# Attention with a top-1 mixture of experts on one core: maxima exchanged in full between the two heads, subtracted with one product per part and head, and a third maxima job moved in three iterations

## The chip, the cores and the metric

The kernel runs on one core of a Trainium2 chip. The metric is device time in microseconds for one execution, inputs and outputs in the chip's main memory. The engines are PE (matrix products), DVE (vector work), ACT (activations and copies), POOL (a general engine, which here also issues some transfers) and SP (which issues most transfers). "PEld" in the profile is PE's loading of weights, which runs beside its products.

## The reference

Attention over 8 batches, 8 heads, 576 positions and 64 dimensions, with a mask by blocks of 64: a query sees its own block and all earlier ones. The result, seen as rows of 512, goes through a layer in which each row uses one of 8 experts.

```
scores = (q @ k.T) / sqrt(64)
scores = where(block_i >= block_j, scores, -1e9)
scores = scores - max(scores, axis=-1)
attn   = exp(scores);  attn = attn / (sum(attn) + 1e-9)
x      = attn @ v                      # as rows of 512
logits = x @ w_gate;   local = sigmoid(x @ w_local)
e      = argmax(logits[s]) if s == 0 or local[s] < 0.5 else the previous row's e
out[s] = softmax(logits[s])[e] * (relu(x[s] @ w1[e]) @ w2[e])
```

## The kernel before

The attention is a software pipeline over 32 pairs of heads. One pair lies on the 128 partitions, head 0 on 0 to 63 and head 1 on 64 to 127 (a "half" each). In the iteration numbered `it` (L869) pair a = it + 2 is turned (PE transposes queries and keys, L912), pair c = it + 1 gets its scores and exponentials, pair e = it is multiplied with v (`av`), and pair x = it - 1 is normalized, stored, and used for the gate's logits. The order on each engine is written out by hand: an engine takes its instructions in the order of the code, and an instruction that waits holds all behind it.

Scores are made transposed: keys on the partitions, queries along the columns (`products`, L554), in four segments of one or two parts (`SEGS`, L366). A query's maximum therefore has to be subtracted along the columns. It is found beforehand from a low-precision copy of queries and keys (`qh`, `kh`) with queries on the partitions: `top` makes the products and `maxima` reduces them on DVE, in three jobs per pair. Jobs 0 and 1 treat query blocks 6 and 7, 4 and 5, 0 and 1 by pairs of blocks: such a product has block b on partitions 0 to 63 and block b + 1 on 64 to 127, for each head h in a column of its own. Job 2 treats blocks 8, 3 and 2 with `qd`, a block-diagonal arrangement that has head 0 on the lower and head 1 on the upper partitions from the start. All jobs write into the tile `mx`; `PLACE` (L505) says where a block's columns begin.

To subtract, `shift` (L545, on POOL) spreads a column of `mx` over a diagonal (`negi` is minus the identity), and `less` (L558) adds ones-times-diagonal to the scores on PE, which puts minus the maximum of a query in its column on all key partitions. Each half of the partitions serves one head: `lhsT=ones[rows(h)]`, `rhs=diag[rows(h), ...]`.

For jobs 0 and 1 half of the maxima lie on the other head's partitions. L538 copies these to columns 6 to 8 of the right partitions: two copies of 64x3, on DVE (for the first pair on ACT). The diagonals of such blocks are then in two places, the direct ones and the copied ones, in an order that alternates with the head, so that `less` uses separate products: L573 for blocks 2, 3 and 8, and L583 for the others, each half and each of the two places by itself. That makes 34 small products per pair, 22 in the first two segments and 12 in the others; `shift` treats 12 places in three calls (4, 5 and 3).

Around it on DVE: the maxima of job 1 (L535) and the copies (L538) end an iteration; at the head of the next stand the normalization of pair x (`norm`, L481 and L482), what the plan has for "begin", the maxima of job 2 (L543), and the casts into `kh`, `qh` (L928) and `qd` (L939). On PE the head has job 2's products (L526), the eight transposes (L912), the turning of pair x's result (`turn_x`, L620), then scores. Job 2 reads the old `kh` and `qd`, so the casts follow its products. All three jobs share one PSUM tile for their products (`ps_m`): the next job's products wait for the last job's maxima. On POOL the order is: shifts of job 1, the issue of one load of expert weights (L64), shift of job 2, the cast of the result for storing (L464), and tails of `kh` and `qd` (L976, L978).

The routing of the rows (which expert, which place) is done in small steps in the middle of the attention; `plan` (L826) says in which iteration and where. For groups g = 0, 1, 2 the iteration 8g + 11 has "begin" (`ranks_in`), "turn" (`ranks`) and "mid" (`shares`) steps, all on DVE.

After the attention the experts' layer runs over tiles of 128 rows (gather, L744, L756, scatter).

Of the kernel before, what the change touches and what calls it, by code (L numbers as in the profile page):

```python
# [16 lines left out]
def kernel(  # L17
# [11 lines left out]
    nc = tc.nc  # L29
    F32 = mybir.dt.float32  # L30
    BF16 = mybir.dt.bfloat16
# [4 lines left out]
    ALU = mybir.AluOpType  # L36
# [365 lines left out]
    with tc.manual_schedule():  # L402
# [6 lines left out]
        def const(shape, dt, name):  # L409
            return cst.tile(shape, dt, tag=name, name=name)  # L410
# [17 lines left out]
            nc.gpsimd.memset(vt[i][:, :, :, D:D + 1], 1.0)  # L428
            nc.gpsimd.memset(vt[i][64:128, 4], 0.0)

        diag0 = scr[:, 0:12 * 64].rearrange("p (s t) -> p s t", t=64)
        diag1 = const([P, 12, 64], BF16, "diag")
        nats, pls, mxs, xs, xbs, xTs = {}, {}, {}, {}, {}, {}

        def load_qk(i, engs=(nc.sync,)):
# [59 lines left out]
        def rows(h):  # L495
            return slice(64 * h, 64 * h + 64)
# [33 lines left out]
        def maxima(i, job, ps):  # L530
            flat = ps.rearrange("p b c -> p (b c)")
            mx = mxs[i]
            if job < 2:
                for (b, c, n) in PAIRS[job]:
                    nc.vector.reduce_max(mx[:, PLACE[b]:PLACE[b] + 2], ps[:, :, c:c + n], axis=AX)  # L535
                if job == 1:
                    for h in range(2):
                        (nc.vector.tensor_copy if i else nc.scalar.copy)(  # L538
                            mx[rows(h), 6:9], mx[rows(1 - h), h:6:2])
                return  # L540
            for (b, c, n) in FULL:
                z = PLACE[b]
                nc.vector.reduce_max(mx[:, z:z + 1], flat[:, c:c + n], axis=AX)  # L543

        def shift(i, s0, n):  # L545
            nc.gpsimd.tensor_tensor(  # L546
                (diag1 if i else diag0)[:, s0:s0 + n, :], negi[:, None, :].to_broadcast([P, n, 64]),
                mxs[i][:, s0:s0 + n, None].to_broadcast([P, n, 64]), op=ALU.mult)

        def products(i, ps, s, part):  # L550

# [6 lines left out]
        def less(i, ps, s, part):  # L558

            j, a, n, c = SEGS[s][part]  # L560
            diag = diag1 if i else diag0
            blocks = range(a // 64, (a + n) // 64)
            ends = part == len(SEGS[s]) - 1
            for b, w in ((0, 1), (2, 2), (4, 2), (8, 1)):
                if b not in blocks:
                    if b == 4 and 6 in blocks:
                        b, w = 6, 1
                    else:
                        continue
                o, z = c + 64 * b - a, PLACE[b]  # L570
                if b in (2, 8):
                    for h in range(2):
                        nc.tensor.matmul(ps[:, h, o:o + 64 * w], lhsT=ones[rows(h), :],  # L573
                                         rhs=diag[rows(h), z:z + w, :], start=False,
                                         stop=ends and b + w - 1 == blocks[-1])
                    continue
                for e in range(2):
                    for h in range(2):
                        out_s = ps[:, h, o:o + 128 * w].rearrange("p (m e t) -> p m e t", e=2, t=64)
                        zz = slice(z + h, z + h + 2 * w - 1, 2)  # L580
                        if e:
                            zz = slice(6 + z // 2, 6 + z // 2 + w)
                        nc.tensor.matmul(out_s[:, :, e ^ h, :], lhsT=ones[rows(h), :],  # L583
                                         rhs=diag[rows(h), zz, :], start=False,
                                         stop=ends and e == 1 and b + 2 * w - 1 == blocks[-1])

        def seg_tile():
            return ps_sp.tile([P, 2, 512], F32, tag="s", name="ps_s")
# [239 lines left out]
        def at(it, where, f):  # L828
            plan.setdefault((it, where), []).append(f)

        for g in range(3):
            i0 = 8 * g + 9
            at(i0, "turn", lambda ps, g=g: fresh(g))
            at(i0, "turn", lambda ps, g=g: fresh_b(g))
            at(i0, "free", lambda ps: rows_ps(ps, buf))
            at(i0, "mid", lambda ps: scan_rows(plan["free"], buf))
            at(i0, "end", lambda ps: ends_ps(ps, buf))
            at(i0 + 1, "begin", lambda ps: carry(ps, buf))
            at(i0 + 1, "turned", lambda ps: carry_ps(ps, buf))
            at(i0 + 1, "turn", lambda ps: scanned(ps, buf))  # L840
            at(i0 + 1, "first", lambda ps, g=g: chosen_ps(g, ps, buf))
            at(i0 + 1, "mid", lambda ps, g=g: chosen(g, ps))
            at(i0 + 1, "end", lambda ps, g=g: ranks_ps(g, ps))
            at(i0 + 2, "begin", lambda ps: ranks_in(ps))
            at(i0 + 2, "turn", lambda ps, g=g: ranks(g))
            at(i0 + 2, "mid", lambda ps, g=g: shares(g))
            at(i0 + 3, "turn", lambda ps, g=g: ranks_b(g))
            at(i0 + 3, "mid", lambda ps, g=g: shares_b(g))
            at(i0 + 4, "top", lambda ps, g=g: shares_out(g))
            at(i0 + 4, "turn",  # L850
               lambda ps, g=g: low((ohl01[:, GC * g:GC * g + GC, :] if g < 2 else ohl1), GC * g, GC))
# [17 lines left out]
        for it in range(-2, NPR):  # L869
# [11 lines left out]
                                      in_=moe_w_local[ko * P:(ko + 1) * P, :])  # L881

            last_ps = None
            if on_c and c > 0:
                last_ps = top(c, 2, ps_mp) if c > 1 else second
            if last_ps is not None and not on_a:
                maxima(c, 2, last_ps)
                shift(c, 9, 3)
            if on_x:
                norm(x, g0_b, 0, 6)  # L890
            run(it, "top")
            run(it, "begin", ge)
            if last_ps is not None and on_a:
                maxima(c, 2, last_ps)
                shift(c, 9, 3)
            if on_x:
                store_x(x, nc.gpsimd.tensor_copy if it < NPR - 1 else nc.scalar.copy)
            if it == NPR - 1:
# [2 lines left out]
            if on_a:  # L901
                nat = nats[a]
                if a < 3:
                    pw = [g_tile(0), g_tile(1)]
                else:
                    ps = ps_sp.tile([P, 2, 512], F32, tag="s", name="ps_t")
                    pw = [ps[:, 0, :], ps[:, 1, :]]
                pl = pls[a] = plb[:, a % 2]
                mxs[a] = o_p.tile([P, 12], F32, tag="mx", name="mx")
                for w in (1, 0):  # L910
                    for t in range(4):
                        tr = nc.tensor.transpose(pw[w][:, 128 * t:128 * t + 128],  # L912
                                                 nat[:, 4 * w + t].rearrange("p h d -> p (h d)"),
                                                 id_f)
                        if w == 0 and a:

                            tc.declare_no_dep(tr.ins, group="keys", reason="another bank")
                    if a == 0:
                        warm(8 if w else 0)
                        turned(0, w, pw[w])  # L920
                        continue
                    if a < 3:
                        continue
                    cp = nc.scalar.copy(pl[:, w * S:w * S + 512], pw[w])  # L924
                    if w == 1:
                        tc.add_to_no_dep_group("keys", cp.ins)
                    src = pl[:, w * S:w * S + 512]
                    nc.vector.tensor_copy(kh[:, 0:512] if w else qh, src)  # L928
                if a in (1, 2):

                    cast = nc.scalar.copy if a == 1 else nc.vector.tensor_copy
                    cast(kh[:, 0:512], pw[1])
                    cast(qh, pw[0])
                    src = qh
                    for w in (1, 0):
                        nc.scalar.copy(pl[:, w * S:w * S + 512], pw[w])
                if a:
                    for h in range(2):
                        nc.vector.tensor_copy(  # L939
                            qd[rows(h), 0:2, rows(h)],  # L940
                            src[rows(h), 128:256].rearrange("p (b t) -> p b t", t=64))
# [69 lines left out]

            if a == 1:
                maxima(a, 1, top(a, 1, ps_mp))
                shift(a, 0, 4)
                shift(a, 4, 5)
            elif on_a:
                maxima(a, 0, top(a, 0, ps_mp))
            if on_x and not on_a:
# [26 lines left out]
            if on_a:  # L1045
                if a != 1:
                    maxima(a, 1, top(a, 1, ps_mp if a else ps_sp))
                    shift(a, 0, 4)
                    shift(a, 4, 5)
                if a == 0:  # L1050

                    opened = seg_tile()
                    products(a, opened, 0, 0)
                    products(a, opened, 0, 1)
                    maxima(a, 2, top(a, 2, ps_mp))
                    shift(a, 9, 3)
            if it >= 0:

                for _ in range(2 if it in (4, 6) else 1):
# [179 lines left out]
```

## Time and profile before

| | |
|---|---|
| median of 3 runs | 488.1 us (486.54 to 491.87) |
| the profiled execution | 487.98 us, span 486.2 us |
| PE busy | 469.7 us, 97% |
| DVE busy | 343.4 us, 71% |
| POOL busy | 267.5 us, 55% |
| ACT busy | 252.3 us, 52% |
| the products that subtract maxima | L573 x448, L583 x640 |
| shifts on POOL (L546) | 59.5 us x93, and three of the first pair |
| the copies on DVE (L538) | 18.1 us x62 |

The attention takes up to about 330 us of the span, the experts' layer the rest. A steady iteration takes about 9.8 us, and more where the gate's sums or the routing have work in it. The span is the time from the first to the last instruction of the program; the execution's time is 1.8 us longer. A matmul's duration in the profile includes its way through the array, so that the distance from one start to the next, and not the duration, says what it costs.

### The profile page before, as it was taken

What the parts mean: (1) busy time and instruction counts of PE and PEld (TensorE: products, weight loads), DVE (VectorE), ACT (ScalarE), POOL (GpSimd) and SP (SyncE); (2) the same over time, 40 slices, a digit from 0 to 9 for tenths busy, and PEclk for the clock granted to TensorE, in tenths of its full rate; (3) what the DMA queues carried; (4) which work ended last, traced back from release to release, by engine and by line L of the source; (5) the groups of instructions that cost most, each with busy time, mean ns of one, the idle gap of its engine ahead of it and who ended that gap; (6) DMA issues with size and microseconds to landing.
All of it is one profiled execution on the core that took longest, in us unless ns stands there. A gap on an engine that the chain in (4) does not pass through costs nothing.

```text
span 486.2 us, 19978 instructions
## 1 busy us (share of the span) xinstructions
PE 469.7 (97%) x7959; PEld 374.7 (77%) x7980; DVE 343.4 (71%) x868; ACT 252.3 (52%) x512; POOL 267.5 (55%) x477
## 2 busy tenths in 40 slices
PE   8999999999999999999999999999999999999992
PEld 6687888888878888887888887878777777676770
DVE  5688767778898887889877879996468953434330
ACT  4645555455545455554555554544545545555551
POOL 3455444544445554444554345354587778888761
PEclk9999999999999999999999999999999999999997
DMA  7787999997999789787888878634556666667541
GB/s 153 137 179 135 167 171 185 187 158 148 172 165 157 149 156 170 147 162 145 138 164 161 166 142 165 104 60 100 122 152 149 132 151 164 145 150 150 149 115 50
DMA packets 180974, 71.33 MB, mean 147 GB/s; under 512 B 165008, under 2 KB 173200, under 8 KB 180880
## 3 DMA queue, kind: packets, MB, share of 16 engines
q1 hardware_dynamic: 161920, 37.93, 38.4%
q0 software_dynamic: 17760, 31.79, 35.1%
q8 instruction: 66, 1.08, 1.0%
q10 hardware_dynamic: 1200, 0.30, 0.3%
q14 instruction: 28, 0.23, 0.2%
HBM read 67.45 MB, written 14.97 MB: 170 GB/s over the span
## 4 chain that ended last, share of the span: by engine, by line
PE 86%; DVE 6%; DMA 2%; issue 2%; POOL 1%; ACT 1%; POOLq 0%; DVEq 0%; ACTq 0%
PE ps_s L554 18%; PE g L614 15%; PE ps_h L744 13%; PE ps_o L756 12%; PE ps_t L912 5%; PE g L606 4%; PE ps_m L526 3%; PE g L620 3%; PE ps_s L583 3%; PE ps_m L515 3%; DMA out_dram<-o_sb,tok2s 2%; DVE mx L535 2%; PE g L663 2%; PE ps_s L573 2%; DVE mx L543 1%
## 5 line engine op out<-in xcount | busy, mean ns | idle before, releaser
L593 ACT ACTIVATE prob<-ps_s 128x640 f32<-128x640 f32 (+2 forms) x128 | 100.2, 834 | 86.7 <-PE ps_s L573 62.7
L554 PE MATMUL ps_s<-plb 64*128 64x320 f32 (+4 forms) x768 | 105.9, 407 | 0.0
L535 DVE TENSOR_REDUCE mx<-ps_m 128x2 f32<-128x1024 f32 (+2 forms) x96 | 80.2, 864 | 32.3 <-PE ps_m L519 32.1
L546 POOL TENSOR_TENSOR diag<-negi,mx 128x256 bf16<-128x256 f32 (+2 forms) x93 | 59.5, 640 | 52.8 <-DVE mx L535 18.1
L614 PE MATMUL g<-vt,prob 128*64 128x65 f32 x2560 | 87.7, 223 | 0.2 <-issue 0.2
L554 PEld LDWEIGHTS ps_s<-plb 64*128 64x128 f32 x768 | 66.8, 186 | 24.8 <-issue 9.6
L598 POOL MEMSET prob<- 64x128 f32 x128 | 23.9, 200 | 108.5 <-ACT prob L593 108.5
L614 PEld LDWEIGHTS g<-vt,prob 128*64 128x64 f32 x2560 | 80.3, 138 | 3.7 <-issue 0.3
L756 PE MATMUL ps_o<-w_bf,hT 128*128 x283 | 67.4, 379 | 1.7 <-issue 0.7
L748 ACT ACTIVATE hT<-ps_h 128x512 bf16<-128x512 f32 x76 | 45.2, 597 | 19.8 <-PE ps_h L744 19.5
L924 ACT COPY plb<-ps_t 128x512 f32<-128x512 f32 x58 | 31.1, 589 | 42.5 <-PE ps_t L912 42.5
L760 ACT ACTIVATE o_sb<-ps_o,share 128x512 f32<-128x512 f32 x38 | 26.1, 687 | 45.8 <-PE ps_o L756 39.8
L756 PEld LDWEIGHTS <-hT 128*128 128x128 bf16 x304 | 28.3, 98 | 27.8
L543 DVE TENSOR_REDUCE mx<-ps_m 128x1 f32<-128x576 f32 (+2 forms) x96 | 43.0, 503 | 3.8 <-PE ps_m L526 3.6
L720 DVE COPY natb<-w_bf 128x4096 bf16 x20 | 24.6, 1228 | 29.9 <-PE ps_h L744 27.4
L720 DVE COPY plb<-w_bf 128x4096 bf16 x20 | 24.5, 1227 | 26.5 <-PE ps_h L744 25.3
L744 PEld LDWEIGHTS <-natb 128*128 128x128 bf16 x608 | 35.5, 98 | 4.6 <-issue 0.3
L744 PEld LDWEIGHTS <-plb 128*128 128x128 bf16 x608 | 35.5, 98 | 4.4 <-issue 0.3
L766 POOL DMA_INDIRECT out_dram<-o_sb,tok x20 | 30.3, 1517 | 13.2 <-ACT o_sb L760 8.2
L766 POOL DMA_INDIRECT out_dram<-o_sb,tok2s x18 | 30.7, 1704 | 11.6 <-ACTq L1191 4.8
L912 PE MATMUL ps_t<-id_f,natb 128*128 128x128 f32 x232 | 30.1, 273 | 0.0
L583 PEld LDWEIGHTS <-ones 64*128 64x128 bf16 x640 | 23.4, 94 | 7.8 <-issue 5.4
(271 smaller groups left out, 827.6 us busy)
## 6 DMA issues: line engine op xcount, KB each, us to landing
w_bf<-in_moe_w_dram POOLq DMA_DIRECT2D x32, 512.0 KB, 6.5
vt<-in_v_dram SPq DMA_DIRECT2D x64, 128.0 KB, 4.0
natb<-in_k_dram SPq DMA_DIRECT2D x63, 128.0 KB, 4.0
natb<-in_q_dram SPq DMA_DIRECT2D x63, 128.0 KB, 3.4
x_rows<-xb SPq DMA_DIRECT2D x32, 128.0 KB, 5.4
natb<-in_k_dram SPq DMA_DIRECT2D x32, 32.0 KB, 2.5
vt<-in_v_dram SPq DMA_DIRECT2D x32, 32.0 KB, 6.5
x_rows<-xb SPq DMA_DIRECT2D x64, 8.0 KB, 3.9
```

What stands on the lines that cost most here:

```text
L535: nc.vector.reduce_max(mx[:, PLACE[b]:PLACE[b] + 2], ps[:, :, c:c + n], axis=AX)
L543: nc.vector.reduce_max(mx[:, z:z + 1], flat[:, c:c + n], axis=AX)
L546: nc.gpsimd.tensor_tensor((diag1 if i else diag0)[:, s0:s0 + n, :], negi[:, None, :].to_broadcast([P, n, 64]), mxs[i][:, s0:s0 + n, None]. ...
L554: nc.tensor.matmul(ps[:, h, c:c + n], lhsT=pls[i][rows(h), S + 128 * j:S + 128 * j + 128], rhs=pls[i][rows(h), a:a + n], start=part == 0, ...
L593: nc.scalar.activation(p[:, :, SEG0[s]:SEG0[s] + w], ps[:, :, 0:w], func=AF.Exp, scale=scale_attn)
L614: nc.tensor.matmul(g[rows(e), o + 65 * h:o + 65 * h + 65], lhsT=p[:, h, c:c + 64], rhs=t[:, j, h, :], start=(j == 0), stop=(j == m))
L720: nc.vector.tensor_copy(w, w1_bf[:, bass.ds(off, WE)])
L744: nc.tensor.matmul(ps_h[:, f, :], lhsT=w[:, ko * F + fo * P:ko * F + fo * P + P], rhs=xb[:, ko * P:(ko + 1) * P], start=(ko == 0), stop=(k ...
L748: nc.scalar.activation(hT[:, half * 4:half * 4 + 4, :], ps_h, func=AF.Relu)
L756: nc.tensor.matmul(ps_o, lhsT=hT[:, fo, :], rhs=w2_bf[:, bass.ds(woff + fo * Dm, Dm)], start=(fo == 0), stop=(fo == FO - 1))
L766: wr = nc.gpsimd.indirect_dma_start(out=out_flat, out_offset=bass.IndirectOffsetOnAxis(ap=g[1][:, g[3]:g[3] + 1], axis=0), in_=o_sb, in_of ...
L912: tr = nc.tensor.transpose(pw[w][:, 128 * t:128 * t + 128], nat[:, 4 * w + t].rearrange("p h d -> p (h d)"), id_f)
```

## The change

The maxima of jobs 0 and 1 are exchanged in full. Three copies in place of two, on POOL (for the first pair on ACT), one after the other: upper-block columns of head 1's lower partitions are parked in columns 6 to 8 of the upper ones, the lower partitions then get head 0's maxima of the upper blocks, and the parked ones go to their place. Then each half of the partitions has all of its head's maxima, block by block. `shift` now takes a block and writes the diagonals in the order of blocks, nine instead of twelve, in four calls per pair (4, 2, 2 and 1 blocks). `less` becomes one product per part and head: 12 per pair in place of 34, over the same columns.

In iterations 11, 19 and 27 (`third_late`) job 2's products, maxima and shifts no longer stand at the head: its products come after the eight transposes, and its maxima before the casts into `kh` and `qh`, which are both made after it. POOL's cast of pair x's result then stands ahead of job 2's shifts.

```diff
-        diag0 = scr[:, 0:12 * 64].rearrange("p (s t) -> p s t", t=64)
-        diag1 = const([P, 12, 64], BF16, "diag")
+        diag0 = scr[:, 0:NB * 64].rearrange("p (s t) -> p s t", t=64)
+        diag1 = const([P, NB, 64], BF16, "diag")
...
                 if job == 1:
-                    for h in range(2):
-                        (nc.vector.tensor_copy if i else nc.scalar.copy)(
-                            mx[rows(h), 6:9], mx[rows(1 - h), h:6:2])
+                    copy = nc.gpsimd.tensor_copy if i else nc.scalar.copy
+                    copy(mx[rows(1), 6:9], mx[rows(0), 1:6:2])
+                    copy(mx[rows(0), 1:6:2], mx[rows(1), 0:6:2])
+                    copy(mx[rows(1), 0:6:2], mx[rows(1), 6:9])
...
-        def shift(i, s0, n):
+        def shift(i, b, n):
+            z = PLACE[b]
             nc.gpsimd.tensor_tensor(
-                (diag1 if i else diag0)[:, s0:s0 + n, :], negi[:, None, :].to_broadcast([P, n, 64]),
-                mxs[i][:, s0:s0 + n, None].to_broadcast([P, n, 64]), op=ALU.mult)
+                (diag1 if i else diag0)[:, b:b + n, :], negi[:, None, :].to_broadcast([P, n, 64]),
+                mxs[i][:, z:z + n, None].to_broadcast([P, n, 64]), op=ALU.mult)
...
-            for b, w in ((0, 1), (2, 2), (4, 2), (8, 1)):
...
+            for h in range(2):
+                nc.tensor.matmul(ps[:, h, c:c + n], lhsT=ones[rows(h), :],
+                                 rhs=diag[rows(h), a // 64:(a + n) // 64, :], start=False,
+                                 stop=part == len(SEGS[s]) - 1)
...
+        third_late = [8 * g + 11 for g in range(3)]
...
-            if on_c and c > 0:
+            if on_c and c > 0 and it not in third_late:
                 last_ps = top(c, 2, ps_mp) if c > 1 else second
...
                 maxima(c, 2, last_ps)
-                shift(c, 9, 3)
+                shift(c, 2, 2)
+                shift(c, 8, 1)
...
-                    nc.vector.tensor_copy(kh[:, 0:512] if w else qh, src)
+                    if it not in third_late:
+                        nc.vector.tensor_copy(kh[:, 0:512] if w else qh, src)
+                if it in third_late:
+                    maxima(c, 2, top(c, 2, ps_mp))
+                    shift(c, 2, 2)
+                    shift(c, 8, 1)
+                    nc.vector.tensor_copy(kh[:, 0:512], pl[:, S:S + 512])
+                    nc.vector.tensor_copy(qh, src)
...
-                    shift(a, 0, 4)
-                    shift(a, 4, 5)
+                    shift(a, 4, 4)
+                    shift(a, 0, 2)
```

More of the change, by code (lines that the diff above doesn't have):

```diff
@@ L561, in less @@
             diag = diag1 if i else diag0
-            blocks = range(a // 64, (a + n) // 64)
-            ends = part == len(SEGS[s]) - 1
-            for b, w in ((0, 1), (2, 2), (4, 2), (8, 1)):
[L565 to L585, printed above, removed]
+            for h in range(2):
+                nc.tensor.matmul(ps[:, h, c:c + n], lhsT=ones[rows(h), :],
+                                 rhs=diag[rows(h), a // 64:(a + n) // 64, :], start=False,
+                                 stop=part == len(SEGS[s]) - 1)
         def seg_tile():
@@ L894 @@
                 maxima(c, 2, last_ps)
-                shift(c, 9, 3)
+                shift(c, 2, 2)
+                shift(c, 8, 1)
             if on_x:
@@ L927 @@
                     src = pl[:, w * S:w * S + 512]
-                    nc.vector.tensor_copy(kh[:, 0:512] if w else qh, src)
+                    if it not in third_late:
+                        nc.vector.tensor_copy(kh[:, 0:512] if w else qh, src)
+                if it in third_late:
+                    maxima(c, 2, top(c, 2, ps_mp))
+                    shift(c, 2, 2)
+                    shift(c, 8, 1)
+                    nc.vector.tensor_copy(kh[:, 0:512], pl[:, S:S + 512])
+                    nc.vector.tensor_copy(qh, src)
                 if a in (1, 2):
@@ L1047 @@
                     maxima(a, 1, top(a, 1, ps_mp if a else ps_sp))
-                    shift(a, 0, 4)
-                    shift(a, 4, 5)
+                    shift(a, 4, 4)
+                    shift(a, 0, 2)
                 if a == 0:
@@ L1055 @@
                     maxima(a, 2, top(a, 2, ps_mp))
-                    shift(a, 9, 3)
+                    shift(a, 2, 2)
+                    shift(a, 8, 1)
             if it >= 0:
```

## The prediction

> **What bounds the kernel now.** I read the page first, then busy time in the attention loop, then the waits of PE, and last the order of time inside single iterations.
>
> ```profile
> span 486.2 us, 19978 instructions
> PE 469.7 (97%) x7959; PEld 374.7 (77%) x7980; DVE 343.4 (71%) x868; ACT 252.3 (52%) x512; POOL 267.5 (55%) x477
> ...
> PE 86%; DVE 6%; DMA 2%; issue 2%; POOL 1%; ACT 1%; POOLq 0%; DVEq 0%; ACTq 0%
> ```
> ```profile
> 25.70:313.70 288.00, 285.90 (x5543) 235.93 (x5540) 236.40 (x617) 153.49 (x337) 138.44 (x338) 1.00 0.86 158
> ```
> ```profile
> PE ps_m L526 <- DVE mx L535: 1.6, 3, 0.6
> ...
> PE ps_m L515 <- ACT qh L933: 0.3, 1, 0.3
> ...
> PE ps_s L573 <- POOL diag L546: 0.2, 1, 0.2
> ```
>
> The reader is to see that PE sets the pace. In the steady loop (second fence: window, its length, then busy PE, PEld, DVE, ACT, POOL) PE is busy 285.9 of 288.0 us at clock 1.00, DVE 236, POOL 138. All 32 iterations are touched, yet only what PE does, or waits for, counts. The third fence lists waits of PE (total, times, longest). All that the change could remove there is 1.6 us behind DVE's maxima and small sums at both ends of the loop.
>
> One plain iteration in order of time (start, duration, engine):
>
> ```profile
> 157.07 1.29 DVE L535 TENSOR_REDUCE mx<-ps_m 128x2 f32<-128x768 f32 x2 [0.98 <-PE ps_m L519]
> 158.18 0.61 POOL L546 TENSOR_TENSOR diag<-negi,mx 128x256 bf16<-128x256 f32 x1 [0.50 <-DVE mx L535]
> 158.40 0.59 DVE L538 COPY mx<-mx 64x3 f32<-64x3 f32 x2
> ...
> 158.97 1.04 PE L912 MATMUL ps_t<-id_f,natb 128*128 128x128 f32 x8
> 159.02 0.20 DVE L481 RECIPROCAL rs<-g 128x6 f32<-128x6 f32 x1
> ...
> 159.25 0.56 DVE L482 TENSOR_TENSOR x<-g,rs 128x384 f32<-128x384 f32 x1
> 159.72 1.34 DVE L543 TENSOR_REDUCE mx<-ps_m 128x1 f32<-128x576 f32 x3
> 159.80 0.75 POOL L64 DMA_DIRECT2D w_bf<-in_moe_w_dram  x1
> 159.96 0.63 PE L620 MATMUL g<-id_f,x 128*128 128x128 f32 x4
> ...
> 161.22 0.54 POOL L546 TENSOR_TENSOR diag<-negi,mx 128x192 bf16<-128x192 f32 x1 [0.67 <-DVE mx L543]
> ...
> 162.51 0.22 PE L573 MATMUL ps_s<-diag,ones 64*128 64x128 bf16 x2
> ```
>
> Two things stand here. The last diagonal is done at 161.22 + 0.54 = 161.76, and PE takes it up at 162.51: 0.75 us to spare. And L620 starts 0.99 us after the eight transposes L912, although another iteration needs less:
>
> ```profile
> 117.87 1.04 PE L912 MATMUL ps_t<-id_f,natb 128*128 128x128 f32 x8
> 118.75 0.60 PE L620 MATMUL g<-id_f,x 128*128 128x128 f32 x4
> ```
> ```profile
> 138.19 1.04 PE L912 MATMUL ps_t<-id_f,natb 128*128 128x128 f32 x8
> ...
> 139.20 0.63 PE L620 MATMUL g<-id_f,x 128*128 128x128 f32 x4
> ```
> ```profile
> issue: 2.3, 14
> ```
>
> That is 0.88 us, with nothing in the way. L620 turns what L482 normalized; L482 ends at 159.25 + 0.56 = 159.81, and L620 follows 0.15 later. So a hidden wait of 0.11 us stands there (0.13 in the iteration at 138.19). The wait table calls it "issue": the last row is L620's own, 2.3 us of idle weight loading in 14 cases, 0.16 each, of which 0.11 delays the matmul.
>
> **The change, part by part.** *One product per part and head.* Per iteration 34 small matmuls become 12; 22 go, 704 in all. The columns stay the same. The two halves run side by side, so the two clusters are 960 and 640 columns long:
>
> ```profile
> 152.70 0.22 PE L573 MATMUL ps_s<-diag,ones 64*128 64x128 bf16 x2
> ...
> 153.12 0.38 PE L515 MATMUL ps_m<-kh,qh 64*128 64x512 bf16 x2
> 153.34 0.20 PE L519 MATMUL ps_m<-ones,unseen 64*128 64x64 bf16 x2
> ```
> ```profile
> 156.31 0.28 PE L583 MATMUL ps_s<-diag,ones 64*128 64x128 bf16 x4
> ...
> 156.59 0.39 PE L515 MATMUL ps_m<-kh,qh 64*128 64x384 bf16 x4
> ```
>
> Start to next start, 22 matmuls take 0.42 us and 12 take 0.28: both 0.44 ns a column. The L515 pair of 512 columns takes 0.22, which is 0.43 ns a column. Columns are paid, not instructions. At 0.43 ns the 1600 columns would take 0.69 of the 0.70 us now: 0.4 us over 32 iterations. If each reading is off by its rounding, a pair may cost up to 6 or 7 ns of its own; 11 pairs fewer would give 2.3 us. I take **0.9 us** (0.42 ns a column, a pair of 512 in 0.215), near the lower end because the L515 row is of the new form. The Trainium skill (TensorE: Matmul & The Clock Gate, "Wait — 56ns, not 53.3ns?") puts a fixed 2.5 ns on each matmul, which for 11 pairs would be 0.9 us too; it also states a floor of about 25 ns from start to start, and the trace, at 0.42 / 22 = 19 ns, is below it because two run at once.
>
> *The exchange leaves DVE.* Two copies (L538, 0.59 us) stood between the maxima, done at 157.07 + 1.29 = 158.36, and the normalization at 159.02. That needs the last products with v, which end here:
>
> ```profile
> 158.12 0.46 PE L614 MATMUL g<-vt,prob 128*64 128x65 f32 x10
> ```
>
> So it can start near 158.65, 0.37 us earlier; L482 then ends near 159.44, and L620 could go at 159.59, before the transposes are through (159.85). The hidden wait vanishes. Of its 14 places 11 are like this one (11 × 0.11 = 1.2) and three like that at 138.19 (3 × 0.13 = 0.4): **1.6 us**. Next in line there is PE itself.
>
> *The exchange and four shifts on POOL.* Three copies chained on each other come before the first shift, and everything behind them waits: shifts, the weight load's issue L64, the last shifts, the cast of the results (whose stores SP issues), then the tails of the keys.
>
> ```profile
> L546 POOL TENSOR_TENSOR diag<-negi,mx 128x320 bf16<-128x320 f32 x31 | 22.4, 723 | 10.9 <-PE ps_m L526 7.6 <-DVE mx L538 2.7 <-DVE rs L481 0.6
> ...
> L978 POOL CAST qd<-plb 64x64 bf16<-64x64 f32 x64 | 19.5, 305 | 1.9
> ...
> L546 POOL TENSOR_TENSOR diag<-negi,mx 128x192 bf16<-128x192 f32 x31 | 18.1, 585 | 23.7 <-DVE mx L543 10.7 <-PE g L963 6.8 <-DMA vt<-in_v_dram 5.3
> ```
> ```profile
> L538 DVE COPY mx<-mx x62: 161/290/504, 15.2 to 323.4; 64x3 f32<-64x3 f32 x62
> ```
>
> Shifts: 320 columns take 0.723 us, 256 take 0.61 (at 158.18): 64 columns more cost 0.11 us, so 128 columns cost 0.39 and 64 cost 0.28. A copy of 64x3 on POOL is nowhere in the trace. Nearest: POOL's 64x64 cast at 0.305 from above, and 0 from below; the same copy on DVE took 0.29. I take 0.25. Chain: 158.4 + 3 × 0.25 = 159.2, + 0.61 + 0.39 = 160.2, + 0.75 for L64 = 160.9. The third maxima, begun about 0.3 earlier, end at 160.8, so POOL is there just in time; 0.39 + 0.28 more is 161.6, against PE at 162.4. **0 us**, hidden by the 0.75 to spare; a copy above 0.5 us, or a starved shift, breaks the cover (rivals).
>
> *Start and end.*
> ```profile
> L538 ACT COPY mx<-mx x2: 192/192/193, 10.0 to 10.3; 64x3 f32<-64x3 f32 x2
> ```
>
> The first pair of heads copies on ACT, three instead of two, 0.19 us each; behind them ACT casts qh, for which PE waits 0.3 us already: **-0.2 us**. In the second last iteration PE waits for the last diagonal (third fence, L573); two shifts in place of one are 0.39 + 0.28 - 0.51: **-0.15 us**.
>
> *Third maxima behind the turns, iterations 11, 19, 27.* From there DVE works without a pause up to the maxima for which PE waits at the next head:
>
> ```profile
> 127.41 0.60 PE L526 MATMUL ps_m<-kh,qd 128*128 128x512 bf16 x4
> ...
> 128.75 1.34 DVE L543 TENSOR_REDUCE mx<-ps_m 128x1 f32<-128x576 f32 x3
> ...
> 130.34 0.73 DVE L928 CAST qh<-plb 128x512 bf16<-128x512 f32 x1
> ```
> ```profile
> 137.76 0.60 PE L526 MATMUL ps_m<-kh,qd 128*128 128x512 bf16 x4 [0.55 <-DVE mx L535]
> ```
> ```profile
> 120.21 1.02 POOL L546 TENSOR_TENSOR diag<-negi,mx 128x192 bf16<-128x192 f32 x1 [0.94 <-DVE mx L543]
> ...
> 120.32 0.41 DVE L928 CAST qh<-plb 128x512 bf16<-128x512 f32 x1
> ```
>
> Moved behind eight transposes, L526 starts at 127.41 + 0.88 = 128.29; the maxima need the first of its products, within the 0.60 us of this row, so they begin at 128.7 to 128.95: 0 to 0.2 later than now, though DVE would be free 0.4 earlier. Against that, POOL's cast of the results (and SP's stores of them behind it) now comes ahead of the shifts and so out of DVE's casts, where qh took 0.73 beside POOL and 0.41 when POOL's shift stretched to 1.02 instead: up to 0.5 earlier. Between -0.6 and +1.6 us for three (the 0.55 is all there is); I take **0**, so that the waits stay.
>
> Sum: 0.9 + 1.6 - 0.2 - 0.15 = 2.15 us off the profiled execution's 487.98 (486.2 of span and 1.8 around it, 0.1 below the median of 488.1): **485.8 us**.
>
> **The rivals.**
> - *Slower: the last diagonal comes too late.* At 120.21 one shift stretched from 0.54 to 1.02 because DVE's casts ran beside it. The page GPSIMD Engine Reference of the Trainium skill (1. Specifications) says that POOL's SBUF interfaces are shared with DVE, contention arising with certain of its modes; the row agrees. If both new shifts are stretched so in each plain iteration (0.67 + 2 × 0.48 = 1.63 from 160.95), they end at 162.6, 0.2 after PE wants them: 29 × 0.2 = 5.8 lost, 2.15 won, **491.6 us**. It decides from 0.07 us of lateness per iteration. For it: the 1.02 is real. Against: the mean over 31 such shifts is 0.585, which has room for about three at 1.02; the rest took 0.54, and there DVE's cast paid. Copies over 0.5 us would act at the same place, and more strongly.
> - *More: the 1.6 us at L526 goes too*, if DVE's chain shortens: **484.2 us**. For it: DVE's casts vary by 0.3. Against: the later L526.
> - *The exchange's going changes nothing*, since the normalization waits for something else; only the merge and the ends are left, 487.98 - 0.9 + 0.35 = **487.4 us**. Against: L481 starts 0.03 after L538's end.
> - *Instructions are paid, not columns*: 0.70 / 34 = 21 ns each, 22 × 21 ns × 32 = 14.5 us, **473.5 us**. By the floor of 25 ns in the Trainium skill's page (TensorE: Matmul & The Clock Gate) it would be 17.6. Against: the equal 0.44 ns a column.
>
> **How the numbers follow.** Forecast 0.59; diagonal late 0.20 (half of it beyond 1%, with copies over 0.5 us); more 0.10; nothing 0.08; instructions 0.03. One per cent, 4.9 us, is about what a measurement of this kernel can tell from no change. Faster by more: the last rival and the upper part of the second, 0.07. Slower by more: half of the first, 0.10. Within: 0.83. The range goes from 482.8 (both bounds of the merge and L526 together: 487.98 - 2.3 - 1.6 - 1.6 + 0.35) to 491.0, most of the way to the late diagonal.
>
> **What would show it.** Right: L573 and L583 make one row of 12 matmuls per iteration, clusters of about 0.41 and 0.27; L620 0.88 after L912 everywhere; no L538 on DVE, three copies of some 0.25 on POOL; the wait at L526 still near 0.5, three times; PE idle for POOL diag only at the end. Wrong: PE waits for POOL's diagonals in the middle of the loop, copies beyond 0.5, or the 0.11 before L620 still there.

## The result and the profile after

The changed kernel takes 485.82 us (median of 22 runs, 484.05 to 493.74) against 488.27 for the kernel before (22 runs): a ratio of 0.9949 with a 95% interval of 0.9926 to 0.9972, 2.5 us faster. 485.8 was forecast. The medians are over all runs, and the ratio leaves out three runs of the changed kernel above 492 us, which ran slower as a whole. On another chip, where both kernels take some 7.5 us longer (493.2 and 495.86 us), the ratio is 0.9955 (0.9926 to 0.9984).

The page of the changed kernel, and its steady loop (window, length, busy PE, PEld, DVE, ACT, POOL):

```profile
span 484.5 us, 18598 instructions
PE 468.5 (97%) x7276; PEld 368.8 (76%) x7276; DVE 327.1 (68%) x806; ACT 252.8 (52%) x513; POOL 271.9 (56%) x602
```
```profile
26.33:310.96 284.63, 283.19 (x4926) 230.85 (x4925) 220.44 (x560) 153.32 (x337) 147.75 (x451) 1.00 0.88 159
```

The span is 1.7 us shorter. PE has some 680 fewer recorded matmuls and yet only 1.2 us less busy time, which already says that instructions were not the price. It is still busy 283.19 of 284.63 us. DVE lost 16 us of work, POOL gained 4.

PE's waits (total, times, longest), for comparison with those shown of before:

```profile
PE ps_s L568 <- POOL diag L551: 0.8, 1, 0.8
...
PE ps_m L515 <- ACT qh L929: 0.5, 1, 0.5
...
PE ps_m L526 <- DVE rs L481: 0.5, 2, 0.2
...
PE ps_m L526 <- DVE mx L535: 0.2, 1, 0.2
```

The 1.6 us at L526 became 0.7; the two small waits at the ends of the loop grew from 0.2 to 0.8 and from 0.3 to 0.5. And the same plain iteration as in the prediction, in order of time:

```profile
156.10 1.29 DVE L535 TENSOR_REDUCE mx<-ps_m 128x2 f32<-128x768 f32 x2 [0.97 <-PE ps_m L519]
...
157.45 0.18 POOL L540 COPY mx<-mx 64x3 f32<-64x3 f32 x1 [0.74 <-DVE mx L535]
...
157.66 0.20 DVE L481 RECIPROCAL rs<-g 128x6 f32<-128x6 f32 x1 [0.27 <-PE g L599]
157.69 0.18 POOL L541 COPY mx<-mx 64x3 f32<-64x3 f32 x1
157.89 0.56 DVE L482 TENSOR_TENSOR x<-g,rs 128x384 f32<-128x384 f32 x1
157.94 0.19 POOL L542 COPY mx<-mx 64x3 f32<-64x3 f32 x1
157.99 1.04 PE L901 MATMUL ps_t<-id_f,natb 128*128 128x128 f32 x8
158.21 0.97 POOL L551 TENSOR_TENSOR diag<-negi,mx 128x256 bf16<-128x256 f32 x2
...
158.86 0.60 PE L605 MATMUL g<-id_f,x 128*128 128x128 f32 x4
159.12 0.75 POOL L64 DMA_DIRECT2D w_bf<-in_moe_w_dram  x1
...
159.89 0.89 POOL L551 TENSOR_TENSOR diag<-negi,mx 128x128 bf16<-128x128 f32 x2
...
161.39 0.58 PE L568 MATMUL ps_s<-diag,ones 64*128 64x448 bf16 x8
...
161.80 0.38 PE L515 MATMUL ps_m<-kh,qh 64*128 64x512 bf16 x2
```

The normalization L481 now waits for PE's last products with v and no longer for copies. The turning of the results (L605) starts 0.87 us after the transposes, here and in every other iteration but the three with the move, where job 2's products stand between. POOL is through with its copies and shifts at 160.78, 0.61 us before PE takes up the last diagonal at 161.39; in the kernel before it was 0.75. The next iteration's transposes start at 167.63, 9.64 us after these; before it was 9.81.

### The profile page after: what moved, and what is told of

Same layout as the page of the kernel before. It is cut to its first block, busy times and chain, and to the rows that moved or that the text cites. A ratio compares the mean times of both kernels' runs of the same rounds, so it can differ in the third digit from the quotient of the medians.

```text
span 484.5 us, 18598 instructions
## 1 busy us (share of the span) xinstructions
PE 468.5 (97%) x7276; PEld 368.8 (76%) x7276; DVE 327.1 (68%) x806; ACT 252.8 (52%) x513; POOL 271.9 (56%) x602
## 4 chain that ended last, share of the span: by engine, by line
PE 68%; POOL 9%; DVE 8%; issue 7%; DMA 4%; POOLq 1%; ACT 1%; DVEq 0%
PE ps_s L559 17%; PE g L599 14%; PE ps_h L729 5%; PE ps_t L901 5%; PE ps_o L741 5%; PE g L591 4%; PE ps_s L568 4%; POOL scr L689 4%; PE ps_m L526 3%; POOL xg L689 3%; PE ps_m L515 3%; DVE mx L535 2%; PE g L605 2%; DMA out_dram<-o_sb,tok2s 2%; POOL out_dram L751 2%
## 5 line engine op out<-in xcount | busy, mean ns | idle before, releaser
L599 PEld LDWEIGHTS g<-vt,prob 128*64 128x64 f32 x2560 | 80.1, 138 | 3.3
L741 PE MATMUL ps_o<-w_bf,hT 128*128 x304 | 71.5, 379 | 0.6 <-issue 0.5
L551 POOL TENSOR_TENSOR diag<-negi,mx 128x256 bf16<-128x256 f32 (+1 forms) x124 | 58.5, 491 | 10.0 <-DVE mx L546 5.7
L751 POOL DMA_INDIRECT out_dram<-o_sb,tok x20 | 24.9, 1244 | 16.2 <-ACT o_sb L745 13.4
L568 PE MATMUL ps_s<-diag,ones 64*128 64x448 bf16 (+1 forms) x372 | 31.5, 274 | 0.8 <-POOL diag L551 0.8
L901 PE MATMUL ps_t<-id_f,natb 128*128 128x128 f32 x232 | 30.1, 273 | 0.0
L591 PEld LDWEIGHTS g<-vt,prob 128*64 128x64 f32 x640 | 21.2, 137 | 7.2 <-issue 6.2
```

What stands on the lines that cost most here:

```text
L551: nc.gpsimd.tensor_tensor((diag1 if i else diag0)[:, b:b + n, :], negi[:, None, :].to_broadcast([P, n, 64]), mxs[i][:, z:z + n, None].to_b ...
L568: nc.tensor.matmul(ps[:, h, c:c + n], lhsT=ones[rows(h), :], rhs=diag[rows(h), a // 64:(a + n) // 64, :], start=False, stop=part == len(SE ...
L599: nc.tensor.matmul(g[rows(e), o + 65 * h:o + 65 * h + 65], lhsT=p[:, h, c:c + 64], rhs=t[:, j, h, :], start=(j == 0), stop=(j == m))
L741: nc.tensor.matmul(ps_o, lhsT=hT[:, fo, :], rhs=w2_bf[:, bass.ds(woff + fo * Dm, Dm)], start=(fo == 0), stop=(fo == FO - 1))
L901: tr = nc.tensor.transpose(pw[w][:, 128 * t:128 * t + 128], nat[:, 4 * w + t].rearrange("p h d -> p (h d)"), id_f)
```

## The experiments

All are edits of the changed kernel, and each ratio is with the kernel before on the same chip. The total of a run scatters by some us, mostly behind the attention: from the first product of the experts' layer to the end it is 153.3 to 157.6 us in the traces of the first four runs below, which were on one chip, and 152.0 to 152.8 in the four on another. What an edit does inside the attention is read more sharply from the distance between two transposes (L901, or the same line under another number), which repeats to 0.02 us in plain iterations.

**The subtraction in 34 products again.**

```diff
+        PIECES = {(128, 448): [(0, 128), (128, 128), (256, 128), (384, 64)], (512, 64): [(0, 64)],
...
-            for h in range(2):
-                nc.tensor.matmul(ps[:, h, c:c + n], lhsT=ones[rows(h), :],
-                                 rhs=diag[rows(h), a // 64:(a + n) // 64, :], start=False,
-                                 stop=part == len(SEGS[s]) - 1)
+            for (o, m) in PIECES[(a, n)]:
+                for h in range(2):
+                    nc.tensor.matmul(ps[:, h, c + o:c + o + m], lhsT=ones[rows(h), :],
+                                     rhs=diag[rows(h), (a + o) // 64:(a + o + m) // 64, :],
+                                     start=False,
+                                     stop=part == len(SEGS[s]) - 1 and o + m == n)
```

`PIECES` lists for each part where its pieces of 64 and 128 columns begin and how long they are; the cut leaves out the other parts.

> The changed kernel with the subtraction cut into 17 pairs of products again (34 small ones, over pieces of 64 and 128 columns as before, each adjacent), diagonals as in the changed kernel. Theory (columns are paid, with 2 to 3 ns for a pair): the two clusters take 0.42 and 0.28 us again, a plain iteration 9.67 in place of 9.64, total 0.9 us more, about 486.7. Rival (instructions are paid, 21 ns each): 0.45 us an iteration, 500 us.

Ratio 0.9977 (0.9956 to 0.9998). A plain iteration of this run, PE alone:

```profile
157.82 1.04 PE L908 MATMUL ps_t<-id_f,natb 128*128 128x128 f32 x8
161.22 0.59 PE L574 MATMUL ps_s<-diag,ones 64*128 64x128 bf16 x22
161.65 0.38 PE L515 MATMUL ps_m<-kh,qh 64*128 64x512 bf16 x2
...
167.49 0.38 PE L908 MATMUL ps_t<-id_f,natb 128*128 128x128 f32 x2
```

22 products take 0.43 us from start to next start, where 8 take 0.41 in the changed kernel; the iteration is 9.67 in place of 9.64. Columns are paid, and a piece costs almost nothing of its own. 0.03 us in each of 32 iterations is the 0.9 us of the forecast; the rival of 21 ns an instruction would have shown 0.45 us in each.

**The copies on DVE.**

```diff
-                    copy = nc.gpsimd.tensor_copy if i else nc.scalar.copy
+                    copy = nc.vector.tensor_copy if i else nc.scalar.copy
```

> The changed kernel with its three copies on DVE instead of POOL (the first pair stays on ACT). Theory (what the change won beside the merge is that the normalization no longer waits for copies on DVE): three copies of 0.29 us put the normalization 0.6 us later, of which 0.27 is spare, so a plain iteration goes from 9.64 to about 10.0 us, and the turning of the results starts about 1.25 us after the eight transposes in place of 0.87; 14 plain iterations and three behind the routing steps: about 6 us, 492 us. Rival (it doesn't matter where the copies stand): a plain iteration at 9.64, 485.8 us.

Ratio 0.9982 (0.9955 to 1.0009). The direction is that of the theory, but the interval overlaps that of the changed kernel. The loop settles it, and there the expected size was wrong.

```profile
157.20 0.16 DVE L540 COPY mx<-mx 64x3 f32<-64x3 f32 x1
...
157.40 0.17 DVE L541 COPY mx<-mx 64x3 f32<-64x3 f32 x1
157.59 0.17 DVE L542 COPY mx<-mx 64x3 f32<-64x3 f32 x1
157.76 1.04 PE L901 MATMUL ps_t<-id_f,natb 128*128 128x128 f32 x8
157.79 0.20 DVE L481 RECIPROCAL rs<-g 128x6 f32<-128x6 f32 x1
...
158.73 0.63 PE L605 MATMUL g<-id_f,x 128*128 128x128 f32 x4
```
```profile
167.52 0.27 PE L901 MATMUL ps_t<-id_f,natb 128*128 128x128 f32 x1
```

The three copies take 0.59 us together and not three times the 0.29 of a copy in the kernel before: here they take 0.16 to 0.17 each and stand 0.19 apart. So the normalization starts as late as before, L605 comes 0.97 us after the transposes, and the iteration is 9.76. Against 9.64, the place of the copies is worth 0.12 us in a plain iteration, where about 0.36 was expected. L605 is late by this much in 16 iterations, some 1.9 us in all.

The 0.29 was the mean of two unlike copies. In the kernel before, in the iteration that the prediction shows:

```profile
158.40 0.42 DVE L538 COPY mx<-mx 64x3 f32<-64x3 f32 x1
...
158.83 0.16 DVE L538 COPY mx<-mx 64x3 f32<-64x3 f32 x1
```

The first one runs beside POOL's shift of 256 columns, which goes from 158.18 to 158.79, and ends 0.02 us after it; beside the second POOL does nothing. It is so in all 31 pairs of copies on DVE: the first ends 0.02 to 0.03 us behind a shift of 0.61 us, the second takes 0.16. In the run with the copies on DVE the shifts wait for all three, so none runs beside them. These rows say that the shift holds the copy up; no run takes the two apart. What stands between PE and its next work is DVE's order, whatever is cheaper elsewhere.

**Without the move in iterations 11, 19 and 27.**

```diff
-        third_late = [8 * g + 11 for g in range(3)]
+        third_late = []
```

> The changed kernel with the third maxima job at the head in all iterations again; exchange and single products stay. Theory of the prediction (the move starts DVE's maxima later and takes POOL's result cast out of DVE's casts, the two cancel): in iteration 11 the third maxima start some 0.5 us earlier than in the changed kernel, kh, qh and qd casts together take about 2.0 us instead of 1.5, PE's wait at the head of iterations 12, 20 and 28 stays at 0.2 to 0.4 us each; total within 1 us of the changed kernel (about 485.8). Rival (the move is what cut these waits from 1.6 to 0.7 us in total): the three waits come to 1.5 us or more again, total about 486.7.

Ratio 0.9925 (0.9897 to 0.9953). From the transposes of iteration 18 to those of iteration 21, first in the kernel before, then in the changed one, then without the move:

```profile
200.04 0.49 PE L912 MATMUL ps_t<-id_f,natb 128*128 128x128 f32 x3
```
```profile
231.32 0.38 PE L912 MATMUL ps_t<-id_f,natb 128*128 128x128 f32 x2
```
```profile
198.51 0.38 PE L901 MATMUL ps_t<-id_f,natb 128*128 128x128 f32 x2
```
```profile
229.30 0.27 PE L901 MATMUL ps_t<-id_f,natb 128*128 128x128 f32 x1
```
```profile
197.00 0.27 PE L901 MATMUL ps_t<-id_f,natb 128*128 128x128 f32 x1
```
```profile
227.56 0.27 PE L901 MATMUL ps_t<-id_f,natb 128*128 128x128 f32 x1
```

31.28, 30.79 and 30.56 us: here the move costs 0.23 us. Around the other two moves (from the transposes of iterations 10 and 26 to those of 12 and 28) it is 20.10 and 19.98 us with the move and 19.80 without, which makes 0.7 in all. The same three iterations as above are longer there by more, 31.62 against 30.55 and 31.10 against 30.56, and the first are even longer than in the kernel before (31.28), because of waits further on. The larger stands in iteration 12 before a product of the gate's sums, and the profile shows nothing that it waits for:

```profile
146.84 0.43 PE L648 MATMUL g<-xT,wgl 128*32 128x128 f32 x8 [0.55 <-issue]
```

The other run of the changed kernel has it too (0.70), the run with 34 products, which has the move as well, does not. So it is not put down to the move, and its cause stays open.

The rival, which wanted 1.5 us of waits at the three heads again, is excluded. Without the move PE's wait there is not 0.5 us but 0.15, a little under the 0.2 to 0.4 of the theory. Why, the third maxima and the next head show, in the changed kernel and then without the move, with its row of waits (the third is just too short to be listed):

```profile
127.62 1.35 DVE L546 TENSOR_REDUCE mx<-ps_m 128x1 f32<-128x576 f32 x3 [0.50 <-PE ps_m L526]
...
136.25 0.60 PE L526 MATMUL ps_m<-kh,qd 128*128 128x512 bf16 x4 [0.23 <-DVE mx L535]
```
```profile
126.58 1.34 DVE L546 TENSOR_REDUCE mx<-ps_m 128x1 f32<-128x576 f32 x3
...
135.48 0.60 PE L526 MATMUL ps_m<-kh,qd 128*128 128x512 bf16 x4
```
```profile
PE ps_m L526 <- PE g L599: 0.3, 2, 0.2
```

The row names PE's own products with v, but those do not hold L526 up: in the plain iteration shown above it starts at 157.54, before they are through at 157.61. It is DVE's last maxima: they are done at 135.34, and L526 starts 0.14 later; with the move they are done at 136.10, and it starts 0.15 later. With the move DVE, on whose unbroken chain this depends, stands idle 0.50 us for products that PE makes later, and the third maxima begin 0.59 us later, counted from the transposes of iteration 10. What the move gives back is smaller: the casts into `kh`, `qh` and `qd` take from 128.89 to 130.41, 1.52 us, with the move and from 127.85 to 129.64, 1.79 us, without it. That fits POOL's cast of the results being out of their way: the last cast into `qd` takes 0.60 us beside it and 0.22 behind it. 0.59 - 0.27 = 0.32 is what the head comes later here, and the transposes behind it come 0.30 later (20.10 against 19.80). Around the other two moves the casts take 1.43 us, and less is lost. What shortened the chain against the kernel before was the exchange's leaving DVE: the normalization at its start comes 0.42 us earlier, counted from the same transposes.

**The move in the iterations at whose head PE waits.**

```diff
-        third_late = [8 * g + 11 for g in range(3)]
+        third_late = [8 * g + 12 for g in range(3)]
```

> The changed kernel with the third maxima job behind the turns in iterations 12, 20 and 28 instead of 11, 19 and 27, which are the ones at whose head PE waits for DVE. Theory (that wait is then covered by 0.87 us of transposes): no wait of PE for the maxima at the products of the third job, 0.5 to 0.7 us less than the changed kernel, about 485.2. Rival (DVE's chain is late anyway and the wait moves to where PE needs its next result): the same time as the changed kernel, with a new wait in these iterations.

Ratio 0.9966 (0.9928 to 1.0004), which does not tell it from the changed kernel. The waits of PE for POOL's diagonals in it, and the place of one:

```profile
PE ps_s L568 <- POOL diag L551: 2.5, 3, 1.2
```
```profile
138.50 0.85 POOL L464 CAST xb<-x 128x576 bf16<-128x576 f32 x1 [0.33 <-DVE mx L546]
...
139.32 0.82 POOL L551 TENSOR_TENSOR diag<-negi,mx 128x128 bf16<-128x128 f32 x2
...
140.19 0.58 PE L568 MATMUL ps_s<-diag,ones 64*128 64x448 bf16 x8 [0.55 <-POOL diag L551]
```

The wait at the head is covered in all three, as the theory said, but in two of them a new one stands in its place, as the rival said: POOL's cast of the results goes ahead of the last shifts, and they are done 0.55 us too late. The 2.5 us of the first row are this wait, one of 1.16 in iteration 28, and the 0.77 at the end of the loop, which has nothing to do with the edit; iteration 20 has none.

**More copies on POOL.** To see how much POOL has to spare, copies into scratch columns that nothing reads were added behind the exchange, three or five:

```diff
                     copy(mx[rows(1), 0:6:2], mx[rows(1), 6:9])
+                    for _ in range(3 if i else 0):
+                        copy(mx[rows(1), 6:9], mx[rows(0), 1:6:2])
```

> The changed kernel with three more copies of 64x3 on POOL behind the three of the exchange (into the scratch columns; nothing reads them). Theory (POOL has 0.6 us to spare before PE needs the last diagonal, in a plain iteration): 0.74 us more on POOL make the last diagonal 0.1 to 0.25 us late, a plain iteration 9.75 to 9.9 us in place of 9.64, PE waits for POOL's diagonals in the middle of the loop; total 2 to 6 us more than the changed kernel. Rival (POOL's work is covered by the weight load's wait or by more than 1 us): 9.64 us as before.

> As the run with three more copies, with five. Theory: 1.22 us more on POOL, 0.6 of them spare, a plain iteration of about 10.2 us, total some 15 us more than the changed kernel. Rival: 9.64 us as before, or a loss far under the part beyond 0.6 us, as PE's later start also lets DVE and the rest move.

One run each, on one chip: 494.9 us with three and 507.7 with five, where the changed kernel gave 493.2 (its runs lie between 491.5 and 501.96, so that a single 494.9 does not tell the two apart). Iteration 2 with three, and with five:

```profile
36.04 1.04 PE L903 MATMUL ps_t<-id_f,natb 128*128 128x128 f32 x8
45.73 1.04 PE L903 MATMUL ps_t<-id_f,natb 128*128 128x128 f32 x8
```
```profile
36.86 1.04 PE L903 MATMUL ps_t<-id_f,natb 128*128 128x128 f32 x8
47.17 1.04 PE L903 MATMUL ps_t<-id_f,natb 128*128 128x128 f32 x8
```

9.69 and 10.31 us, against 9.64. With five copies the loss is as expected (14.5 us). With three it is smaller than the 0.1 to 0.25 us foreseen: 0.05 at most in plain iterations, most of the rest in single ones (PE waits 0.60 in each of the three with the move, 0.49 in iteration 7 and 1.35 in the second last). The reason is not a larger cover. In iteration 2 of the changed kernel the last diagonal is done 2.83 us behind the start of the transposes, and PE takes it at 3.40: 0.57 to spare. With three copies it is done at 3.39 and with five at 4.02. Three copies put it back by 0.56 and not by 0.74, because the last two shifts then take 0.70 us in place of 0.89; with five the room is used up and what lies beyond it is paid in every iteration. This is the mechanism of the prediction's slower rival, shown with its threshold of some 0.6 us.

**The move undone, and both ends of the loop.** From the runs above: the job at the head everywhere, the first pair's copies on POOL, and in the second last iteration the weight load issued behind the last shifts.

```diff
-        third_late = [8 * g + 11 for g in range(3)]
+        third_late = []
...
-                    copy = nc.gpsimd.tensor_copy if i else nc.scalar.copy
+                    copy = nc.gpsimd.tensor_copy
...
                 maxima(c, 2, last_ps)
                 shift(c, 2, 2)
                 shift(c, 8, 1)
+                if it == NPR - 2:
+                    load_weights(halves.pop(0))
...
-            if it >= 0:
+            if it >= 0 and it != NPR - 3:
```

> The changed kernel with three edits: the third maxima job at the head in all iterations (as in the run without the move), the first pair's three copies on POOL in place of ACT, and the weight load that POOL issued ahead of the last diagonals of the second last iteration issued behind them. Theory (what the change lost is at these three places): 0.2 us for each of three moves, 0.3 us at the start (PE waits 0.3 us for qh in place of 0.54), 0.5 us at the second last iteration (PE waits 0.2 us for the diagonal in place of 0.77): 1.4 us less than the changed kernel. Rival (these waits are taken up again behind them): the experts' layer starts at the same time as in the changed kernel.

> The changed kernel itself, unaltered, beside the next ones. Expected by every theory: plain iterations of 9.64 us as before, 0.4 to 0.6% less than the kernel before.

On one chip: the unaltered changed kernel 493.2 us, ratio 0.9955 (0.9926 to 0.9984), and this one 491.97, ratio 0.9928 (0.9898 to 0.9958). The intervals overlap, so 1.2 us less is the expected size and sign but is not settled by the totals. In the attention it is plain: from the second last iteration's issue and its last diagonal,

```profile
320.43 0.65 POOL L551 TENSOR_TENSOR diag<-negi,mx 128x128 bf16<-128x128 f32 x2 [0.44 <-DVE mx L546]
...
321.02 0.81 POOL L64 DMA_DIRECT2D w_bf<-in_moe_w_dram  x1
321.13 0.58 PE L568 MATMUL ps_s<-diag,ones 64*128 64x448 bf16 x8 [0.30 <-POOL diag L551]
```

PE waits 0.30 there in place of 0.77. The three routing groups, counted as above, take 30.82, 30.55 and 30.55 us, where the changed kernel on this chip took 31.69, 30.78 and 31.10; part of the first difference is the open wait of iteration 12. At the start the edit gave less than the 0.3 us expected:

```profile
10.12 1.04 PE L903 MATMUL g<-id_f,natb 128*128 128x128 f32 x8
...
13.04 0.59 PE L568 MATMUL ps_s<-scr,ones 64*128 64x448 bf16 x8 [0.28 <-POOL scr L551]
...
14.55 1.62 PE L559 MATMUL ps_s<-plb 64*128 64x320 f32 x8 [0.36 <-ACT prob L578]
```

PE no longer waits for `qh`, but for the first pair's diagonals and then for its exponentials, and the transposes of iteration 0 come at 17.01, against 16.92 in the changed kernel, which had come to the first row's place earlier, at 9.63. The run with five more copies, whose start is that of the changed kernel, came there at 10.10 and to iteration 0 at 17.14: about 0.15 us is what the edit gives. The experts' layer starts 1.93 us earlier than in the changed kernel (336.27 against 338.20), so the rival falls; how much of it reaches the end, the scatter of that layer hides.

## Why the prediction was right, and where its terms were off

The time was right to 0.1 us, and its two main steps were right in kind and near in size. That the sum came out so close is also luck: three terms were off, and single waits that nobody forecast took up what they left over.

- **One product per part and head, 0.9 us: right.** Iterations without any wait went down by 0.03 us, and cutting the products up again adds 0.03.
- **The wait before the turning of results, 1.6 us: right, a little more.** L605's own table no longer has the 14 idle stretches, and the distance from the transposes is 0.87 us. A plain iteration with this wait lost 9.81 - 9.64 = 0.17 us, of which 0.03 is the merge: 0.14 where 0.11 was forecast, some 2.0 us over 14. The run with the copies on DVE brings most of it back, 0.12.
- **POOL's added work at 0: right in the loop.** A copy took 0.18 us and they stand 0.25 apart, as assumed. The two small shifts took 0.46 and 0.43 on the mean rather than 0.39 and 0.28, DVE's casts beside them; that lies inside the cover. In the three iterations with the move the cover is used up: in iteration 11 the last diagonal is done at 130.09 (129.09 + 1.00), and PE takes it at 130.14. This costs nothing by itself, since the next head waits for DVE anyway.
- **Start, -0.2 us: right.** Three copies on ACT put `qh` back, PE's wait for it went from 0.3 to 0.5, and the next iteration ran 0.25 longer.
- **Second last iteration, -0.15 us: too small.** PE's wait for the diagonal went from 0.22 to 0.77. The prediction counted the split shift and left out that copies ahead of the weight load's issue push it against the last shift. The two shifts also took 0.81 there and not 0.67. Issued behind, the wait is 0.30.
- **The third job's move at 0, the waits at L526 to stay: wrong.** The waits fell from 1.6 to 0.7 us. The bounds were right: counted from the transposes of iteration 10, the third maxima began 0.17 us later than in the kernel before (11.05 against 10.88; 0 to 0.2 was forecast), and the casts took 0.39 to 0.47 less (up to 0.5 was forecast). The step that failed is to let the two cancel. It also took the exchange and the move together: without the move the three waits are 0.15 each, against 0.55 before, and the move takes back 0.7 us in all.

Of the rivals, the late diagonal did not come in plain iterations of the changed kernel, though its cover is as thin as it was put; L526's wait went in part, and goes down to 0.15 without the move; that the exchange's going changes nothing is excluded by the run with the copies on DVE, and that instructions are the price by the run with 34 products.

The terms as measured come to some 3.0 us (0.9 + 2.0 + 0.9 at L526, less 0.25 at the start and 0.55 at the end). In the profiled executions the experts' layer starts 2.31 us earlier (335.81 against 338.12), and the medians show 2.45. Single waits lie between, such as the open one in iteration 12. In the profiled execution of the changed kernel 1.1 us went to a wait of the experts' layer for a transfer, which the other run of it does not have.

## What to carry to other kernels

Where one engine is busy through the loop, read the distance from one of its starts to the next rather than its durations: it shows hidden waits, here 0.11 to 0.14 us before a step, that tables of waits put down to "issue", and it shows what many small products cost beyond a few large ones over the same columns, here 0.03 us for 22 more. Work taken off an engine that the bound engine waits on pays even if the engine that takes it is slower, as long as that one's spare time, measured where its last result is due, covers it. A mean over unlike instructions is no price for the next one: look at each with what runs beside it. A reordering that puts a product later for the sake of one queue should be tried without it: here it idled the engine that the next step depended on.

## What was not expected of the hardware

- A copy of 64x3 on DVE took 0.16 to 0.17 us where POOL did nothing beside it, and 0.42 in the kernel before where POOL's shift ran; there it ended 0.02 to 0.03 us behind the shift in 31 of 31 cases. So the copies' 0.59 us on DVE was in part POOL's doing.
- Beside DVE's casts a shift of 64 columns on POOL took 0.43 us on the mean, and 0.28 at the least; DVE's casts took 1.43 to 1.52 us with less of POOL's work beside them and 1.79 with more.
